# A Fourier mixer with a low-rank token mixer and an MLP: a new opening for batch 0, and a new plan for batches 1 and 2

## The chip, the cores and the metric

The kernel runs on one core of a Trainium2 chip. The core has a matrix engine (TensorE, PE), a vector engine (VectorE, DVE), an engine for activations and copies (ScalarE, ACT), a general one (GpSimd, POOL), and a queue engine (SyncE, SP) that only issues DMAs. Each runs its own instructions in order and waits on semaphores. The time is the device time of one execution in microseconds; the number given is the median of the runs.

## The reference, cut to what matters

```python
X = np.fft.rfft(x, axis=1)                  # x: 8 x 3136 x 256, along the 3136 tokens
Y = X * (filt_r + 1j * filt_i)[None]        # filters: 1569 x 256
y = np.fft.irfft(Y, n=3136, axis=1)
h = y.transpose(0, 2, 1) @ U @ V            # rank 32, U: 3136 x 32, V: 32 x 3136
u = y + h.transpose(0, 2, 1)
out = u + np.maximum(u @ w_ch1, 0) @ w_ch2  # 256 -> 1024 -> 256
```

Inputs and output are float32; the kernel computes in float16 with float32 accumulation.

## The kernel before, in words

The 3136 tokens are 64 q by 49 r, and both transforms are done as matmuls in two factors, so that each batch goes through four stages. **Step 1** (`st1`, lines 262 to 290) multiplies x by a 64-point transform, 13 pieces for each batch, and stores the result in the DRAM tensor `ct1`. The **middle stage** loads tiles `a2` (98 rows, eight tiles k of four frequencies each) from `ct1`, applies the 49-point transform (`stage2`, two matmuls with `w2t`), multiplies by the filter, applies the inverse 49-point transform (`stage3`), casts to `esb` and stores to `ct2`. The filter product has two forms. In the first, `fa` and `fc` hold rearranged copies of the filters; three products and a sum give `y`, and stage 3 needs one matmul for each half tile. In the second, stage 2 is done with two weight sets, one product with `fb` as loaded gives `uv`, and stage 3 adds two matmuls for each half tile. **Low rank** (`low_rank`, `low_rank_end`) multiplies `esb` by the transformed U (`uh`, from `u_hat`) to a 32-row `h1`. **Stage 4** (`stage4`) takes `e2`, 64 rows of the middle result read back from `ct2` with `h1` beneath them as rows 64 to 95 (`put_h`), and multiplies by `sv`, which holds the inverse 64-point transform and V, to the transposed tokens `ut` of one group. Then the MLP: `mm1`, a ReLU on ScalarE into a ring `hring`, `mm2_part`, the residual, `och` and the output.

There are six groups of 512 tokens for each batch and one of 128 for each pair of batches. The last loop runs over groups and eight steps t in each: `mm1` of group n, at two of the steps `stage4` of group n+1, and a quarter or half of `mm2` of group n-1. Into these steps a table written by hand (`plan`, `early`) puts everything that the next batches need: `plan_mid` the middle stage, `plan_st1` step 1, `plan_rest` the loads of `e2`, low rank and `put_h`. A step number counts over all groups; batch 1's groups start at step 48. The tables set the order within each engine, and nothing reorders it at run time.

Before the loop, batch 0 takes a path of its own. Step 1 stays on the chip: `turned` writes it transposed into `cm`, `turn_a2` transposes it back into the tiles that stage 2 wants, and `mid_first` runs 16 half tiles j in the second form of the product, four of them on GpSimd. After it come low rank, all of step 1 of batch 1, and stage 4 of group 0. In this version `cm` is the memory of `fc`, so that the rearranged filters (`make_fa`) are made after batch 0.

Loads that convert float32 to float16 are issued by GpSimd (x, filters, U, V, `w1sb`, `w2sb`). In the order of the built program each of them waits until the one eight places ahead of it has landed. SyncE issues the others, in order; a load from `ct1` or `ct2` waits there for the stores that it reads, and everything behind it waits as well. [...]

Of the kernel before, what the change touches and what calls it, by code (L numbers as in the profile page):

```python
# [24 lines left out]
def _consts():  # L25
# [10 lines left out]
    wf = np.zeros((128, 25, 128))  # L36
    for h in range(2):
        wf[h::2, 0:24, 64 * h:64 * h + 64] = t1[:, 24 * h:24 * h + 24]
    wf[0:64, 24, 0:64] = t1[:, 48]
# [59 lines left out]
    return (wf.reshape(128, 25 * 128).astype(f16), w2.astype(f16), g3.astype(f16),  # L99
# [4 lines left out]
def kernel(  # L104
# [13 lines left out]
    names = ("wf", "w2", "g3", "s4", "su", "tw", "kr")  # L118
    wf_d, w2_d, g3_d, s4_d, su_d, tw_d, kr_d = (
# [22 lines left out]
    def bank(tag):  # L142
        of = {"m": (0, 1), "o": (2, 3), "w": (4,), "e": (7,), "f": (0, 1, 2, 3, 4, 7), "e0": (7, 4), "f0": (0, 1), "w1": (7, 5, 6)}[tag]
        turn[tag] = turn.get(tag, -1) + 1
        return psum[:, of[turn[tag] % len(of)], :]


    NH = 17
    hring = cst.tile([128, NH, 512], F16, name="hring")
# [3 lines left out]
    wf = cst.tile([128, 25, 128], F16, name="wf")  # L153
    for c in range(4):
        i = slice(8 * c, min(8 * c + 8, 25))
        nc.sync.dma_start(wf[:, i], wf_d.rearrange("p (i m) -> p i m", m=128)[:, i])
# [3 lines left out]
    def load_x(b, c, after=None):  # L160
# [3 lines left out]
        else:  # L164

            t = sb.tile([128, 4, XW], F16, tag="x", bufs=4, name="x")
            if after is not None:
                nc.gpsimd.tensor_copy(t[0:1, 0, 0:1], after[0:1, 0:1])
# [10 lines left out]
    def load_filters(a, z):  # L179
# [8 lines left out]
        if z == NK:  # L188
            for p0, src in ((0, filt_r), (64, filt_i)):
                nc.gpsimd.dma_start(fb[p0 + 25:p0 + NR, 31, :],  # L190
                                    dram(src.tensor, 32 * DM, [[64 * DM, 24], [1, DM]]))
            nc.gpsimd.dma_start(fb[0:25, 31, :], dram(filt_r.tensor, 0, [[64 * DM, 25], [1, DM]]))
            nc.gpsimd.dma_start(fb[65:89, 31, :],
                                dram(filt_i.tensor, 64 * DM, [[64 * DM, 24], [1, DM]]))
            nc.gpsimd.dma_start(fb[64:65, 31, :],
                                dram(filt_r.tensor, 1568 * DM, [[DM, 1], [1, DM]]))

    zero = cst.tile([128, 64], F16, name="zero")
    nc.vector.memset(zero, 0.0)
    nc.vector.memset(fb[96:128], 0.0)  # L200
    nc.scalar.copy(fb[32:64].rearrange("p s (k f) -> p (s k) f", f=64),
                   free(zero, 32, 64, 0, [[0, NK * DM // 64], [1, 64]]))
    nc.vector.memset(fc[:, 24:29, :], 0.0)
    usb = hflat[0:64, 0:NR * RANK]
    nc.gpsimd.dma_start(usb, moe_U.rearrange("(q r) p -> q (r p)", q=NQ))
# [4 lines left out]

# [7 lines left out]
    nc.scalar.dma_start(g3, g3_d.rearrange("p (f m) -> p f m", f=6))  # L218

# [3 lines left out]
    w2sb = cst.tile([128, 8, DM], F16, name="w2sb")  # L223
    vnat = hflat[64:96, 4704:4704 + SEQ]
    nc.gpsimd.dma_start(vnat, moe_V)
    nc.gpsimd.dma_start(w1sb, moe_w_ch1.rearrange("(h dd) c -> dd h c", h=2))

    sv = cst.tile([96, SEQ], F16, name="sv")
    kr = cst.tile([128, 96], F16, name="kr")

    def keep_warm(n):
        z = bank("f")
        for _ in range(n):
            nc.tensor.matmul(z, wf[:, 0, :], wf[:, 0:4, :].rearrange("p i m -> p (i m)"),
                             start=True, stop=True)
# [4 lines left out]
    def u_hat():  # L240
        ud = hflat[0:64, 1568:4704].rearrange("q (p c r) -> q p c r", c=2, r=NR)
        for p, eng in ((0, nc.vector.tensor_copy), (16, nc.scalar.copy)):
            eng(ud[:, p:p + 16], bass.AP(tensor=usb.tensor, offset=usb.offset + p,
                                         ap=[list(usb.ap[0]), [1, 16], [0, 2], [RANK, NR]]))
        for p in range(0, RANK, 8):
            z = bank("f")
# [4 lines left out]
            t = [sb.tile([98, NK, 8], F32, tag=tag, bufs=3, name="ut") for tag in ("ta", "tb")]  # L251
# [8 lines left out]
    def st1(b):  # L260
        for c in range(3):
            asb = sb.tile([128, 8, DM], F16, tag="asb", bufs=3, name="asb")
            for j in range(4):
                pf = bank("w" if b > 1 else "w1")
# [5 lines left out]
                if b == 1 and j % 2:  # L270
                    nc.vector.tensor_copy(dst, pf)
                else:
                    nc.scalar.copy(dst, pf)  # L273
                if j < 3:
                    yield
            for h in range(2):
                nc.sync.dma_start(dram(ct1[b], (16 * c + h) * 64 * DM,
                                       [[DM, 64], [128 * DM, 8], [1, DM]]), asb[64 * h:64 * h + 64])
            if 1 < b < NB - 1 and c:
                load_x(b + 1, c - 1)  # L280
            yield
        pf = bank("w" if b > 1 else "w1")
        nc.tensor.matmul(pf[0:64, 0:DM], wf[0:64, 24, 0:64], xt[b, 3], start=True, stop=True)
        al = sb.tile([64, DM], F16, tag="al", bufs=2, name="al")
        nc.scalar.copy(al, pf[0:64, 0:DM])
        nc.sync.dma_start(dram(ct1[b], 48 * 64 * DM, [[DM, 64], [1, DM]]), al)
        if 1 < b < NB - 1:
            load_x(b + 1, 2)
            load_x(b + 1, 3)
        yield  # L290


    cm = fc.rearrange("p s d -> p (s d)")

    def turned(c):
        for g in range(0, 8 if c < 3 else 1, 4):
# [268 lines left out]
    for n, _ in enumerate(st1(1)):  # L565
        if n == 3:
            low_rank_end(0)
# [200 lines left out]
```

## Time and profile before

| | us |
|---|---|
| median of 10 runs | 557.36 (552.26 to 560.26) |
| profiled execution | 557.31, span 555.5 |
| TensorE busy | 517.3 (93%) |
| ScalarE, VectorE, GpSimd busy | 391.0, 352.8, 282.3 |
| first stage 3 cast (`esb`) of batch 0 | 29.89 |
| last stage 3 cast of batch 0 ends | 50.47 |
| first `mm1` of group 0 | 61.36 |
| first `mm1` of step 8 (group 1) | 72.20 |
| `e2` of batch 1 there, first `stage4` on it | 130.34 |

Times within the execution count from the start of the span. The chain is followed back from the last instruction to what released each one. A wait of an engine that is not on that chain costs nothing by itself. [...]

### The profile page before, as it was taken

The page shows a single profiled execution, that of the slowest core. Times are in us where ns is not written, and L with a number is a line of the kernel's source. Part 1 is how long each engine was busy: PE and PEld are TensorE (multiplying, and loading weights), DVE is VectorE, ACT ScalarE, POOL GpSimd, SP SyncE. Part 2 cuts the span into 40 slices and gives each one's busy share as a digit, 9 for nine tenths or more (in the row PEclk, how much of TensorE's full clock was granted, in tenths as well). Part 3 has the DMA queues.
Part 4 walks back from the last instruction along what each step waited for, and adds up shares of the span by engine and source line. Part 5 has one row for each costly group of instructions (what it writes and reads, how often), then busy time and mean ns, then how long its engine had stood idle before and what let it go on. Part 6 is the DMA issues. An engine that isn't in the chain of part 4 may idle for free.

```text
span 555.5 us, 11638 instructions
## 1 busy us (share of the span) xinstructions
PE 517.3 (93%) x4491; PEld 375.5 (68%) x4491; DVE 352.8 (64%) x409; ACT 391.0 (70%) x684; POOL 282.3 (51%) x194
## 2 busy tenths in 40 slices
PE   4967689996999999999999999999999999999996
PEld 2634356664767777677776777677786777777775
DVE  6654775755756686758746785858746887643332
ACT  8566868774787687767876788667777577765663
POOL 5678179951884065915683175806563297300000
PEclk8798899997999999999999999999999999999999
DMA  9998986894679467774879468765653554343212
GB/s 188 162 163 174 241 151 185 209 229 131 169 186 246 129 174 198 172 200 141 200 220 221 123 173 225 165 197 155 188 170 120 141 167 121 106 113 114 96 77 87
DMA packets 85433, 92.06 MB, mean 166 GB/s; under 512 B 6742, under 2 KB 69417, under 8 KB 85377
## 3 DMA queue, kind: packets, MB, share of 16 engines
q1 hardware_dynamic: 67968, 75.12, 45.8%
q0 software_dynamic: 16960, 15.91, 19.1%
q8 instruction: 35, 0.57, 0.4%
q10 hardware_dynamic: 448, 0.28, 0.3%
q14 instruction: 22, 0.17, 0.1%
HBM read 57.42 MB, written 49.77 MB: 193 GB/s over the span
## 4 chain that ended last, share of the span: by engine, by line
PE 70%; POOL 10%; DMA 7%; DVE 7%; ACT 3%; issue 2%; DVEq 0%; ACTq 0%; POOLq 0%; SPq 0%
PE psum L521 25%; PE psum L488 24%; PE psum L352 4%; PE psum L344 4%; PE psum L477 4%; PE psum L497 3%; PE psum L266 3%; POOL y L634 3%; DMA x<-in_x_dram 3%; POOL x L170 2%; DVE ut L482 1%; DMA w1sb<-in_moe_w_ch_dram 1%; DVE tb L632 1%; PE psum L416 1%; DMA ct<-esb 1%
## 5 line engine op out<-in xcount | busy, mean ns | idle before, releaser
L492 ACT ACTIVATE hring<-psum 128x512 f16<-128x512 f32 (+1 forms) x416 | 237.7, 576 | 103.1 <-PE psum L488 101.9
L488 PE MATMUL psum<-ut,w1sb 128*128 128x512 f16 (+1 forms) x832 | 240.9, 371 | 4.5 <-DVE ut L482 2.1
L521 PE MATMUL psum<-w2sb,hring 128*128 128x256 f16 x1536 | 231.0, 273 | 0.0
L634 POOL TENSOR_TENSOR y<-ta,tb 128x1024 f16<-128x1024 f16 x56 | 120.6, 2160 | 159.5 <-DVE tb L632 113.5
L521 PEld LDWEIGHTS <-hring 128*128 128x128 f16 x1536 | 143.4, 98 | 62.9 <-issue 3.0
L482 DVE CAST ut<-psum 128x512 f16<-128x512 f32 x96 | 71.0, 740 | 107.1 <-PE psum L477 86.8
L488 PEld LDWEIGHTS <-w1sb 128*128 128x128 f16 x832 | 104.7, 145 | 26.9 <-issue 10.2
L529 DVE COPY och<-psum 128x512 f32<-128x512 f32 x96 | 66.2, 689 | 47.3 <-PE psum L497 46.7
L326 ACT CAST esb<-psum 98x512 f16<-98x512 f32 x128 | 74.8, 587 | 22.6 <-PE psum L344 17.0
L628 DVE TENSOR_TENSOR ta<-psum,fb 128x1024 f16<-128x1024 f32 x41 | 50.0, 1219 | 7.9 <-PE psum L352 6.9
L273 ACT CAST asb<-psum 128x512 f16<-128x512 f32 x78 | 45.9, 589 | 12.4 <-PE psum L266 11.3
L497 PE MATMUL psum<-idn,ut 128*128 128x128 f16 x392 | 54.0, 219 | 0.0
L477 PEld LDWEIGHTS <-e 96*128 96x128 f16 x768 | 35.9, 98 | 25.6 <-issue 10.3
L630 DVE TENSOR_TENSOR tb<-psum,fc 64x1024 f16<-64x1024 f32 x41 | 50.3, 1226 | 0.9
L632 DVE TENSOR_TENSOR tb<-psum,fc 64x1024 f16<-64x1024 f32 x41 | 49.9, 1218 | 0.8
L477 PE MATMUL psum<-sv,e 96*128 96x64 f16 x768 | 38.8, 194 | 6.6 <-DMA e<-ct 3.8
L344 PE MATMUL psum<-y,g 128*98 128x512 f16 x105 | 39.9, 380 | 3.0 <-POOL y L634 1.6
L497 PEld LDWEIGHTS <-ut 128*128 128x128 f16 x392 | 38.5, 98 | 4.9
L628 POOL TENSOR_TENSOR ta<-pc,fb 128x1024 f16<-128x1024 f16 x15 | 32.4, 2157 | 10.8 <-ACT pc L638 10.8
L352 PE MATMUL psum<-a,w2t 98*128 98x512 f16 x113 | 34.7, 383 | 2.1 <-DVE tb L632 1.6
L266 PE MATMUL psum<-x,wf 128*128 128x256 f16 x168 | 32.4, 284 | 2.0 <-ACT asb L273 0.6
L630 POOL TENSOR_TENSOR tb<-pc,fc 64x1024 f16<-64x1024 f16 x15 | 31.8, 2122 | 1.2
(93 smaller groups left out, 371.0 us busy)
## 6 DMA issues: line engine op xcount, KB each, us to landing
out_dram<-och SPq DMA_DIRECT2D x47, 512.0 KB
ct<-esb SPq DMA_DIRECT2D x64, 196.0 KB
x<-in_x_dram POOLq DMA_DIRECT2D x48, 256.0 KB, 8.4
e<-ct SPq DMA_DIRECT2D x48, 256.0 KB
a<-ct SPq DMA_DIRECT2D x56, 196.0 KB
ct<-asb SPq DMA_DIRECT2D x42, 256.0 KB
wf<-wf SPq DMA_DIRECT2D x3, 256.0 KB
w1sb<-in_moe_w_ch_dram POOLq DMA_DIRECT2D x1, 512.0 KB, 7.7
```

The costliest lines, as they stand in the source:

```text
L326: nc.scalar.copy(esb[b, k][:, 2 * half:2 * half + 2, :].rearrange("p s d -> p (s d)"), pe[0:98])
L344: nc.tensor.matmul(pe[0:98], g3[:, m, :], v, start=(n == 0), stop=(n == len(parts) - 1))
L477: nc.tensor.matmul(pu[:, 64 * i:64 * i + 64], e2[b, c][:, i, 128 * dh:128 * dh + 128], sv[:, 64 * r:64 * r + 64], start=(i == 0), stop=Tru ...
L482: nc.vector.tensor_copy(o, v)
L488: nc.tensor.matmul(ph[:, 0:n], w1sb[:, dh, :, t], gr.ut[:, dh, 0:n], start=(dh == 0), stop=(dh == 1))
L492: nc.scalar.activation(h[:, 0:n], ph[:, 0:n], RELU)
L497: nc.tensor.matmul(o[:, dh * 128:dh * 128 + 128], gr.ut[:, dh, t0:t0 + n], idn, start=False, stop=(dh == 1), skip_group_check=True)
L521: nc.tensor.matmul(o, gr.h[tt][:, i * 128:(i + 1) * 128], w2sb[:, tt, :], start=(tt == 0), stop=False, skip_group_check=True)
L529: nc.vector.tensor_copy(gr.och[:, 2 * y:2 * y + 2, :].rearrange("p j d -> p (j d)"), gr.pc)
L628: eng.tensor_mul(ta, p, va)
L630: eng.tensor_mul(tb[0:64], p[64:128], vb[64:128])
L634: nc.gpsimd.tensor_add(ys[k], ta, tb)
```

## The change

It has these parts.

- **Constants.** U is loaded by SyncE as float32, and so is `wfc`, a compact form of the step 1 weights from which VectorE builds `wf` with two multiplications. `sv` and `kr` are loaded later. Two constants are new: `sel` and `s4x`.
- **Rows.** Filter products, `y`, `uv` and stage 3 work on 113 rows (NZ) instead of 128. `tb` becomes three fixed tiles whose rows 32 to 63 are zeroed once.
- **cm** is memory of its own, so `fc` can be filled during batch 0: `make_fc` on GpSimd, `make_neg` on VectorE, `make_fa` once batch 1 no longer needs `fb` as loaded.
- **Opening.** `turned` and `u_hat` alternate, and the warm-up matmuls read a zeroed part of `cm`.
- **mid_first.** Only half tile 12 goes to GpSimd; low rank is added up tile by tile; the last filter row is loaded behind `w1sb`; V is reordered by GpSimd between the loads of the first and second third of x of batch 1.
- **Group 0.** Rows 0 to 47 of `e2` come from `ct2`. The other 16 rows are picked from `esb` by 32 selection matmuls (`pick`), into rows that are then multiplied by `s4x`; V times `h1` is a third matmul into the same PSUM tile.
- **Step 1 of batch 1.** Three of its pieces stand in `mid_first`, ten in steps 0 to 7 of the loop. Its odd row (`xl`) is loaded ahead of the last third of x, and `w2sb` behind both. Its last stores are issued by GpSimd.
- **Plan.** Batch 1's middle stage takes tiles in the order 0, 3, 1, 5, 2, 4, 6, 7, four of them in the second form. x of batch 2 is loaded when `a2` of tile 0 has landed, x of batch 3 at steps 40 to 45. Batch 2's middle stage starts at step 44 instead of 39, with its first loads at step 41 instead of 31.

```diff
-    wf = cst.tile([128, 25, 128], F16, name="wf")
-    for c in range(4):
-        i = slice(8 * c, min(8 * c + 8, 25))
-        nc.sync.dma_start(wf[:, i], wf_d.rearrange("p (i m) -> p i m", m=128)[:, i])
+    usb = hflat[0:64, 0:2 * NR * RANK].bitcast(F32)
+    nc.sync.dma_start(usb, moe_U.rearrange("(q r) p -> q (r p)", q=NQ))
+    wfc = hflat[:, 6272:6272 + 1604]
+    nc.sync.dma_start(wfc, wf_d)
...
+    cm = cst.tile([128, 7232], F16, name="cm")
+    nc.vector.memset(cm[:, 2 * SEQ:], 0.0)
...
+    for h in range(2):
+        nc.vector.tensor_scalar_mul(wf[:, :, 64 * h:64 * h + 64],
+                                    wfc[:, 0:1536].rearrange("p (i m) -> p i m", m=64),
+                                    wfc[:, 1600 + 2 * h:1602 + 2 * h].bitcast(F32))
...
+    def make_fc(k, copy):
+        copy(fc[0:NR, 4 * k:4 * k + 4], fb[64:NZ, 4 * k:4 * k + 4])
+
+    def make_neg(k):
+        nc.vector.tensor_scalar_mul(fc[64:NZ, 4 * k:4 * k + 4], fb[64:NZ, 4 * k:4 * k + 4], -1.0)
+
+    def make_fa(k, copy):
+        copy(fa[64:NZ, 4 * k:4 * k + 4], fb[0:NR, 4 * k:4 * k + 4])
...
+        def low_rank_part(k):
+            for i in range(4):
+                a = 4 * k + i
+                nc.tensor.matmul(ph[32 * i:32 * i + 32], uh[:, a, :], esb[0, k][:, i, :],
+                                 start=(k == 0), stop=(k == 7), skip_group_check=True)
...
+        def pick(j):
+
+            for i in range(2):
+                sl = 2 * (j - 12) + i
+                for g in range(4):
+                    nc.tensor.matmul(zp[32 * g:32 * g + 32], sel[:, g, 28 - 4 * sl:60 - 4 * sl],
+                                     esb[0, j // 2][:, 2 * (j % 2) + i, :], start=(sl == 0),
+                                     stop=(sl == 7), skip_group_check=True)
...
+                if k == 5:
+                    load_e2(0, 0, 48)
+                if k == 6:
+                    load_e2(0, 1, 48)
+                if k == 7:
+                    load_e2(0, 1, 64, 48)
+                    nc.sync.dma_start(sv[0:64, 512:], s4_d[:, 512:])
+                    load_e2(0, 2)
+                    load_e2(0, 6)
...
-        for c in range(4):
-            load_x(1, c)
-        nc.gpsimd.dma_start(w2sb, moe_w_ch2.rearrange("(cc t) e -> cc (t e)", t=8))
+        load_x(1, 0)
+        nc.gpsimd.tensor_copy(sv[64:96, :].rearrange("p (r q) -> p r q", q=NQ),
+                              vnat.rearrange("p (q r) -> p r q", q=64))
+        load_x(1, 1)
...
-            if j in (7, 9, 12, 14):
...
+            if j == 12:
+                pc = sb.tile([NZ, 2, 2 * DM], F16, tag="pc", bufs=2, name="pc")
+                nc.scalar.copy(pc, pz[0:NZ])
                 nc.gpsimd.tensor_mul(uv, pc, fin)
+                for k in (3, 2, 5):
+                    make_fc(k, nc.gpsimd.tensor_copy)
             else:
...
+                nc.vector.tensor_mul(uv, pz[0:NZ], fin)
+            if j < 6:
+                turn_a2(j + 2)
             todo.append((j, uv))
-            if len(todo) > 3:
+            while len(todo) > (3 if 11 < j < 15 else 2) or todo and j == 15:
                 do3(*todo.pop(0))
...
+        step1(1)
+        step1(1)
+        pick(14)
+        low_rank_part(7)
+        pick(15)
+        h1[0] = hp = sb.tile([128, DM], F16, tag="hp", bufs=1, name="hp")
+        nc.vector.tensor_copy(hp, ph)
+        zs = sb.tile([128, DM], F16, tag="zs", bufs=1, name="zs")
+        nc.scalar.copy(zs, zp)
+        keep_warm(2, psum[:, 7, :])
+        low_rank_end(0)
...
+                nc.tensor.matmul(pu[dh][:, 64 * i:64 * i + 64],
+                                 e2[0, 0][0:48, i, 128 * dh:128 * dh + 128],
+                                 sv[0:48, 64 * i:64 * i + 64], start=(i == 0), stop=False,
+                                 skip_group_check=True)
+        for dh in range(2):
+            nc.tensor.matmul(pu[dh], zs[:, 128 * dh:128 * dh + 128], s4x, start=False, stop=False,
+                             skip_group_check=True)
+        step1(1)
+        for dh in range(2):
+            nc.tensor.matmul(pu[dh], h1[0][64:96, 128 * dh:128 * dh + 128], sv[64:96, 0:512],
+                             start=False, stop=True, skip_group_check=True)
...
     mid_first()
+    keep_warm(3, psum[:, 7, :])
+    load_x(1, 3)
+    load_x(1, 2)
+    nc.gpsimd.dma_start(w2sb[:, :, 0:DM], moe_w_ch2.rearrange("(cc t) e -> cc t e", t=8))
+    for k in (4, 0, 1, 6, 7):
+        make_fc(k, nc.gpsimd.tensor_copy)
+    put_h(0, 1)
...
+            for k, q in ((0, 11), (3, 11), (1, 11), (5, 11), (2, 17), (4, 20), (6, 22), (7, 25)):
+                at(q, fetch, k)
+            for k, q, d in ((3, 17, 26), (5, 21, 31), (2, 23, 33), (4, 28, 37)):
+                at(q, two, k)
...
+            for k, qs in ((0, (15, 16)), (1, (19, 20)), (6, (33, 34)), (7, (36, 37))):
+                for half, q in enumerate(qs):
+                    at(q, two_q, k, half)
+                    early[q + 1].append((mul_q, (k, half)))
+                    at(q + (3 if k == 7 else 2), three_q, k, half)
+            return 40
...
+    for n in (0, 0, 1, 1, 2, 3, 4, 5, 6, 7):
+        at(n, step1, 1)
+    at(13, lambda: load_x(2, 0, a2q[0][0:1, 0:1]))
+    for c in range(4):
+        if c:
+            at(13 + c, load_x, 2, c)
+        at((40, 42, 44, 45)[c], load_x, 3, c)
...
-            plan_st1(b, 12, (0, 1, 3, 4, 5, 7))
+            plan_st1(b, 18, (0, 3, 4, 5, 7))
...
-        m = later(start[b - 1], (5, -9, -12)[min(b, 3) - 1])
-        z = plan_mid(b, m, (2, 5) if b > 1 else (1, 3, 5))
+        m = later(start[b - 1], (16, -4, -12)[min(b, 3) - 1])
+        z = plan_mid(b, m, (2, 5) if b > 2 else (1, 3, 5))
```

## The prediction

> **What bounds the kernel now.** I read the slices of the page first, then busy time by stretch, then the chain that ended last, then the waits of TensorE, then the instructions in order of time. Two rows of the page (40 slices of 13.9 us; busy share and granted clock of TensorE, in tenths):
>
> ```profile
> PE   4967689996999999999999999999999999999996
> PEclk8798899997999999999999999999999999999999
> ```
>
> From the eleventh slice on TensorE is full at full clock; losses sit in the first six slices and in the tenth. By stretch (us; busy us and count on PE, PEld, DVE, ACT, POOL; clock; DMA share; GB/s):
>
> ```profile
> 0.00:14.00 14.00, 6.44 (x42) 3.73 (x42) 9.62 (x12) 11.16 (x3) 7.74 (x16) 0.84 0.97 188
> 28.00:42.00 14.00, 9.76 (x44) 4.63 (x43) 8.35 (x8) 8.18 (x13) 10.99 (x14) 0.94 1.00 165
> 56.00:70.00 14.00, 9.30 (x60) 4.81 (x59) 10.96 (x18) 11.76 (x14) 3.02 (x6) 0.87 0.92 236
> 126.00:140.00 14.00, 9.76 (x71) 6.34 (x70) 6.84 (x9) 5.89 (x11) 2.30 (x2) 0.76 0.53 145
> 140.00:200.00 60.00, 58.51 (x526) 43.26 (x525) 40.56 (x47) 44.15 (x85) 33.35 (x21) 1.00 0.70 176
> ```
>
> After 140 us TensorE is the bound, and the change hardly touches that work. So the time is: when the group pipeline starts, plus the TensorE work from there, plus stalls before 140 us. The chain (start, length, what) names them:
>
> ```profile
> 5.06 14.35 DMA x<-in_x_dram
> 37.29 0.57 POOL w2sb L384
> 37.87 2.14 POOL uv L397
> 40.05 0.73 PE psum L344 x2
> 48.77 0.61 PE psum L344 x2
> 49.40 0.59 ACT esb L326
> 58.62 1.46 PE psum L234 x6
> 60.35 0.74 DVE ut L482
> 119.92 6.46 DMA ct<-esb
> 126.52 3.68 DMA e<-ct
> ```
>
> x of batch 0 is not in until 19.7. At 37 GpSimd stands at its load of w2sb (3.00 us, until w1sb has landed), so product 7 is late and TensorE idles 3.39 us. The last esb ends at 50.47. Step 1 of batch 1 then runs before group 0, whose first mm1 stands at 61.36, its second half at 62.34. In the loop one wait of TensorE is long, at the turn to batch 1, and matmuls are slow afterwards:
>
> ```profile
> PE psum L477 <- DMA e<-ct: 3.8, 1, 3.8
> ```
> ```profile
> 50.50 0.31 SPq L329 DMA_DIRECT2D ct<-esb  x1
> 53.83 1.11 SPq L438 DMA_DIRECT2D e<-ct  x2
> ```
> ```profile
> 125.37 0.60 PE L521 MATMUL psum<-w2sb,hring 128*128 128x256 f16 x4
> 130.73 1.04 PE L521 MATMUL psum<-w2sb,hring 128*128 128x256 f16 x4
> ```
>
> The SyncE pair shows the price of the round trip through DRAM: 3.33 us from a store to the load that waits for it, 3.7 us more for the load (126.52 to 130.34).
>
> [...] 1.04 for 0.60 us after the wait at 130, until 135.9. [...] The products here take 2.12 us for 1024[...].
>
> **Part by part**, all against this execution (557.31 us, span 555.5; the 1.8 us around it stay; the median of the runs is 557.36).
>
> *Until the first product.* U goes to SyncE (0.74 us less ahead of x on GpSimd), wf is half as large and sv and kr come later: by tile sizes 1.27 MB of constants instead of 1.9 with U. x was 3.2 MB, so 5.1 MB (f32) came in 18.2 us; 0.63 MB less is 2.2 us at that rate, 3 with the earlier issue: x complete near 16.7. But turned and u_hat now alternate on TensorE: 16 turned matmuls 1.9 us (twice) and 1.2, u_hat 1.5+0.75+0.65, warm-up 1.6, from x's first third at 11.5 to 20.5. u_hat's last products and sum on VectorE (1.5), the a2 copy (0.69) and two matmuls (0.43) follow: product 0 at 23.2 instead of 25.45. **-2.2.** The two multiplications that build wf (a 64x2048 scaling takes 0.68) and three memsets (0.5 each) end by 10.5, hidden by x.
>
> *Middle stage of batch 0.* Now 15 products go to VectorE at 1.2, one a2 copy at 0.69, and only product 12 to GpSimd. 113 rows for 128 cost the same[...]. Six rounds also turn a tile: 1.01+0.59 us on ScalarE, so about 1.45 us a round; then 1.2: 23.2+8.7+7.2 is 39.1 after product 11; 13, 14, 15 end at 43.2. Stage 3, two casts and the bank wait put the last esb at 44.5. Before 50.47: **-3.8 more**, the 3.4 us stall at 37 and half a microsecond. GpSimd must be free for product 12 at 39.5: last filters near 26, V reordered 27.5 to 34.5 (6.93), the load of x's second third behind it issued by 35.8. Hidden by 4 us.
>
> *Closing group 0.* Rows 0 to 47 of e2 come from DRAM, 48 to 63 from selection matmuls on esb. These are 32 of the kind of low_rank (32 in 1.06 us), most while TensorE waits. esb of product 11 ends at 41.8; store 3.3 and load 3.7 put e2 at 48.8. [...] I take 47.7. After it 16 matmuls of 64, four of 512, one step 1, three warm-ups and a cast 0.74: 2.4 us at full clock (0.5, 0.86, 0.22, 0.74), 4.4 at half; I take 4.3, since TensorE has stood still before. Full mm1 at 52.0 instead of 62.34. Sum so far **-10.3**, with ends -15 and -8.
>
> *Group 0.* Before, 9.9 us to step 8, with make_fa on ScalarE (3.7) and VectorE in it. Now 10 of 13 pieces of step 1: eight evictions on VectorE 0.69 each, two ut 0.74, put_h, and make_neg, of which three come before step 8 at about 0.35: 9.0 us. **-0.9.** Queued on GpSimd behind product 12: fc copies 3, 2, 5, then x's odd row, the last third, w2sb, five more fc copies, then ct1's last stores. A copy: [...] 2.26 by sv's reorder (6.93 for 3136). [...]
>
> *Steps 8 to 46 of batch 0.* Four of eight k use the two-product form: 16 more matmuls of 512, 3.45 us at 0.216 (pairs of mm1 follow each other in 0.43). VectorE gives up 1.2 us for each and GpSimd two pooled products. a2 of batch 1 waits for ct1's stores on GpSimd: eviction near 60.5, issue and receipt 4.5, load 3.5: 69 against step 15 near 68.5. x of batch 2 is issued only when a2 has landed: 69.5 plus 6 to 8.4, against step 19 near 75.5: 1.5 us late. Against this, half of the four or so microseconds of small waits between 72 and 126 may go: **+3.0** (1.5 to 6).
>
> *Turn to batch 1.* The last stage 3 stays at step 40. a2 of batch 2 is now fetched at step 41 and used at 44, queued on SyncE behind the e2 load that waits for the last ct2 store. The wait moves from e2 at step 46 to a2 at step 44: store 3.3 to 6.5, issue 1, load 3.5, less 5.5 us of steps. That is 2.3 to 5.5 where 3.8 stood: **0** (-2 to +2). Out of cover, each late microsecond counts in full. Batch 2's middle stage has 0.9 us of stage 2 less behind it: **+0.9.** It ends 11 units (512 tokens by one of eight steps) before batch 2's groups, where before it was 14; later batches have 12 and show no such wait: 0.
>
> Sum: -10.3-0.9+3.0+0+0.9 = -7.3; span 548.2, time **550**.
>
> **Rivals.** *A: the start gained is kept and the turn is cheap* (e2 not late, clock full[...]): start 47.5, no late x, turn 3 less: -17, 541. For it: DMA is lighter around 42; against: every round trip measured so far took 7 us. *B: waits in the loop take back the head*: x of batch 2 and a2 each 2 to 3 us late and half clock after each: 556, within half a per cent. For it: both are chained behind GpSimd stores with no slack. *C, slower: GpSimd's queue.* Three fc copies stand ahead of the last third and all eight ahead of ct1's stores, so step 15 moves by eight times a copy's excess over about 1.7 us, and step 4 by three. At 2.26 that is 4.5 us; the gain is gone at 2.6, half a per cent is lost at 3.0: 562. For it: shifting 64 rows down is a form that the trace doesn't show on GpSimd; against: the two-input product takes only 2.12. *D: nothing moves, as the pipeline's start is hidden*: excluded, since after 140 TensorE has no idle time in which a late start could be made up.
>
> **The numbers.** Forecast 0.5 (546 to 555), A 0.22, B 0.16, C 0.12. The range reaches into A and to the end of B: 539 to 560. Faster by over 0.5% (below 554.6; about what a measurement can tell from no change) 0.74, within 0.5% 0.14, slower 0.12.
>
> **What would show it.** Right: first ut cast near 51, no idle time near 37, mm1 of step 8 near 61, four matmuls per k more at the new stage 2 and 3, a TensorE wait for a2 at step 44 and none for e2 at 46. Wrong: first mm1 before 49 (e2's round trip cheaper than 7 us) or after 55; fc copies above 2.3; a wait for x at step 4 or step 19 above 3 us; a new wait at the start of batch 2's groups.

## The result: 1.2% slower, at the turn to batch 1

The changed kernel takes 562.86 us (median of 14 runs, 560.86 to 567.06) against 556.99 us for the kernel before (median of 51, 552.26 to 561.26). The ratio is 1.0116, with a 95% interval of 1.0093 to 1.0140. A ratio here is taken between fast runs alone and so need not be the quotient of the two medians. The forecast was 550.0, so the sign is wrong. The profiled execution of the changed kernel took 561.2 us, its span 559.3 us.

The slices of the changed kernel (40 of 14.0 us; busy share and granted clock of TensorE, in tenths):

```profile
PE   5896889938998999999999999999999999999996
PEclk9899899988999999999999999999999999999999
```

Slices three and five, both 6 before, are 9 and 8 now. But the ninth slice, 112 to 126 us, holds a 3; the worst that the kernel before had at its turn to batch 1 was a 6, one slice later.

By stretch, for the changed kernel (us; busy us and count on PE, PEld, DVE, ACT, POOL; clock; DMA share; GB/s):

```profile
0.00:14.00 14.00, 8.19 (x60) 4.96 (x60) 9.64 (x13) 6.67 (x7) 9.37 (x18) 1.00 0.96 194
28.00:42.00 14.00, 13.20 (x87) 5.69 (x86) 11.59 (x10) 9.11 (x15) 12.67 (x7) 1.00 0.93 177
42.00:56.00 14.00, 9.64 (x94) 5.21 (x94) 6.37 (x9) 6.51 (x12) 9.07 (x11) 1.00 1.05 188
56.00:70.00 14.00, 12.08 (x98) 8.45 (x95) 12.06 (x24) 7.10 (x12) 1.91 (x2) 0.88 0.57 153
112.00:124.00 12.00, 4.88 (x61) 3.54 (x60) 2.11 (x4) 3.57 (x7) 1.94 (x4) 0.87 0.89 173
124.00:136.00 12.00, 7.37 (x49) 4.56 (x49) 5.58 (x7) 2.93 (x6) 0.00 (x0) 0.70 0.54 115
```

The part that the change was about went better than forecast: from 28 to 42 TensorE works 13.20 of 14 us, where it worked 9.76. The loss is in the last two rows, 12.25 us of work in 24 us, the second half of it at a mean clock of 0.70. The kernel before did 18.95 us of work between the same times.

TensorE's longest waits in the changed kernel (what stood, releaser: total, times, longest), and then SyncE's and GpSimd's issues around the worst of them:

```profile
PE psum L399 <- DMA a<-ct: 12.3, 2, 10.0
PE psum L265 <- DVE cm L220: 5.8, 1, 5.8
PE psum L599 <- DMA sv<-s: 2.5, 1, 2.5
```
```profile
110.93 0.56 SPq L658 DMA_DIRECT2D out_dram<-och  x1
112.56 0.32 SPq L376 DMA_DIRECT2D ct<-esb  x1
121.70 0.48 SPq L559 DMA_DIRECT2D e<-ct  x1
122.23 0.59 SPq L559 DMA_DIRECT2D e2l<-ct  x1
122.99 1.31 SPq L362 DMA_DIRECT2D a<-ct  x3
```
```profile
110.94 2.46 POOL L187 DMA_DIRECT2D x<-in_x_dram  x4
113.36 0.58 POOL L180 DMA_DIRECT2D xl<-in_x_dram  x1
```

The last ct2 store of batch 1 leaves at 112.56, and the e2 load that waits for it is issued at 121.70. The time between these two issues is called the receipt of the store from here on. It is 9.1 us, where the kernel before needed 6.6 (119.92 to 126.52). The three a2 loads of batch 2 stand behind that load on the same queue. In the 1.6 us ahead of the store and the 1.4 us after it, GpSimd sends the loads of x(3,1), x(3,2) and xl of batch 3, four times 256 KB and 32 KB. SyncE has just sent 512 KB of output. In the kernel before those loads of x left at 109.4 to 112.4, 7.5 us ahead of the store.

What TensorE saw of it, in order of time (start, length, instruction, idle time before it and its releaser):

```profile
45.56 0.64 PE L517 MATMUL psum<-sv,e 48*128 48x64 f16 x16 [0.85 <-DMA e<-ct]
...
55.72 0.39 PE L599 MATMUL psum<-sv,e 96*128 96x64 f16 x8 [2.47 <-DMA sv<-s]
70.44 0.59 PE L399 MATMUL psum<-a,w2t 98*128 98x512 f16 x2 [2.36 <-DMA a<-ct]
...
126.84 1.01 PE L399 MATMUL psum<-a,w2t 98*128 98x512 f16 x2 [9.96 <-DMA a<-ct]
...
128.93 1.06 PE L643 MATMUL psum<-w2sb,hring 128*128 128x256 f16 x4
...
135.68 0.60 PE L643 MATMUL psum<-w2sb,hring 128*128 128x256 f16 x4
```

The wait of 0.85 us at 45.56 is all that TensorE sees of group 0's round trip through DRAM. The wait of 9.96 us ends at 126.84. After it the same four matmuls take 1.06 us and not 0.60, until about 131. The granted clock is 1.00 at the start of the wait, 0.50 from 121 to 131.2, and 1.00 again from 131.3.

The lead of the changed kernel over the kernel before, read at the same step of the loop in both traces, tells where the time went (us; negative is ahead; for group 0 of the kernel before, the second half of its first mm1 is taken):

```
first full mm1 of group 0     48.10 against  62.34   -14.2
mm1 of step 8                 60.02 against  72.20   -12.2
mm1 of step 44               115.83 against 123.42    -7.6
first stage 4 of batch 1     130.85 against 130.34    +0.5
its fourth full group        168.15 against 168.15     0.0
batch 2's second group       205.93 against 202.55    +3.4
last stage 4                 539.73 against 535.97    +3.8
```

14.2 us are won at the opening. Then 6.6 are lost between group 0 and step 44, 8.1 at the turn, and 3.4 in the half batch before batch 2's groups.

This is one execution of each kernel, and their starts differ from one execution to the next. In the traces of five kernels with the new opening (the changed one and the first four of the experiments below) the first full mm1 of group 0 stands at 46.92 to 49.14 and the mm1 of step 44 at 115.83 to 117.70. In three with the old opening these stand at 59.74 to 62.34 and at 119.83 to 123.42. The pair in the table has the earliest step 44 of the five against the latest of the three. Taken between the means, the lead is 12.6 us at group 0 and 4.6 at step 44. With the 8.1 us of the turn and 2.9 from there to batch 2's second group that makes a kernel 6.4 us slower, which is what the ratio says (6.5 us); the pair of traces alone gives 3.8.

### The profile page after: what moved, and what is told of

It reads as the page before. It is cut to its first block, busy times and chain, and to the rows that moved or that the text cites. A ratio compares the mean times of both kernels' runs of the same rounds, so it can differ in the third digit from the quotient of the medians.

```text
span 559.3 us, 11736 instructions
## 1 busy us (share of the span) xinstructions
PE 519.4 (93%) x4540; PEld 375.2 (67%) x4540; DVE 353.0 (63%) x413; ACT 375.6 (67%) x678; POOL 283.7 (51%) x204
## 4 chain that ended last, share of the span: by engine, by line
PE 55%; POOL 5%; ACT 1%; DVE 1%; issue 1%; ACTq 0%; POOLq 0%
PE psum L643 21%; PE psum L610 21%; PE psum L619 3%; PE psum L599 3%; PE psum L391 3%; PE psum L399 3%; PE psum L304 2%; POOL y L743 2%; POOL x L187 1%; PE psum L537 1%; POOL tb L741 1%; POOL ta L737 1%; POOL tb L739 1%; ACT esb L369 0%; DVE ut L604 0%
## 5 line engine op out<-in xcount | busy, mean ns | idle before, releaser
L743 POOL TENSOR_TENSOR y<-ta,tb 113x1024 f16<-113x1024 f16 x52 | 112.4, 2168 | 160.3 <-DVE tb L741 103.7
L604 DVE CAST ut<-psum 128x512 f16<-128x512 f32 x94 | 69.7, 742 | 98.8 <-PE psum L599 85.6
L737 DVE TENSOR_TENSOR ta<-psum,fb 113x1024 f16<-113x1024 f32 x37 | 45.1, 1218 | 17.8 <-issue 9.8
L399 PE MATMUL psum<-a,w2t 98*128 98x512 f16 x120 | 37.1, 386 | 16.1 <-DMA a<-ct 12.3
L739 DVE TENSOR_TENSOR tb<-psum,fc 49x1024 f16<-49x1024 f32 x37 | 45.4, 1226 | 1.0
L741 DVE TENSOR_TENSOR tb<-psum,fc 49x1024 f16<-49x1024 f32 x37 | 45.1, 1218 | 1.0
L599 PE MATMUL psum<-sv,e 96*128 96x64 f16 x752 | 37.8, 193 | 3.2 <-DMA sv<-s 2.5
L391 PE MATMUL psum<-y,g 113*98 113x512 f16 x98 | 37.4, 381 | 2.9 <-POOL y L743 1.6
L737 POOL TENSOR_TENSOR ta<-pc,fb 113x1024 f16<-113x1024 f16 x15 | 32.3, 2156 | 10.5 <-ACT pc L747 10.4
L739 POOL TENSOR_TENSOR tb<-pc,fc 49x1024 f16<-49x1024 f16 x15 | 31.8, 2119 | 1.2
```

The source lines that it names most:

```text
L391: nc.tensor.matmul(pe[0:98], g3[0:NZ, m, :], v, start=(n == 0), stop=(n == len(parts) - 1))
L599: nc.tensor.matmul(pu[:, 64 * i:64 * i + 64], e2[b, c][:, i, 128 * dh:128 * dh + 128], sv[:, 64 * r:64 * r + 64], start=(i == 0), stop=Tru ...
L604: (nc.scalar.copy if gr is groups[0] and dh else nc.vector.tensor_copy)(o, v)
L737: eng.tensor_mul(ta, p[0:NZ], va)
L739: eng.tensor_mul(tb[0:NR], p[64:NZ], vb[64:NZ])
L743: nc.gpsimd.tensor_add(ys[k], ta, tb)
```

## The experiments

The theory, called T in the expectations: at the turn the loads of x collide with the last ct2 store and stretch its receipt, and all that SyncE holds behind the waiting e2 load is late. Its rivals: the order on SyncE, or the output store ahead, is the cause by itself (O); or the loss is the added work of the loop and the stall only shows where it ends (W). Gains below that are worked out from two ratios are the difference of the ratios to the kernel before, times 557 us; every group of runs had its own runs of the kernel before beside it.

**x of batch 3 held back.**

```
-        at((40, 42, 44, 45)[c], load_x, 3, c)
+        if c == 1:
+            at(42, lambda: load_x(3, 1, e2[1, 0][0:1, 0, 0:1]))   # GpSimd waits for e2(1,0)
+        else:
+            at((40, 42, 44, 45)[c], load_x, 3, c)
```

> Only the loads of x(3,1), x(3,2) and xl of batch 3 change: they are held on GpSimd until e2(1,0) has landed. Theory T (these five loads, 0.8 MB issued at 110.9 to 113.4, stretch the receipt of the last ct2 store of batch 1, issued at 112.6, from some 3.5 to 9.1 us, and everything queued on SyncE behind it is late): the receipt falls to 3.5 to 5 us, TensorE's wait for a2 at step 44 from 10.0 to 4 or 5 us, time 5 to 6 us below the changed kernel. Rival O (the order on SyncE and the 512 KB store of the output ahead make the receipt long anyway): receipt above 7.5 us, wait above 8 us, time within 1.5 us of the changed kernel.

Measured: 554.73 us, ratio 0.9964 (0.9936 to 0.9993), 8.5 us below the changed kernel by the two ratios. SyncE's two issues, and TensorE's wait:

```profile
113.80 0.32 SPq L376 DMA_DIRECT2D ct<-esb  x1
116.49 0.48 SPq L559 DMA_DIRECT2D e<-ct  x1
```
```profile
121.31 1.01 PE L399 MATMUL psum<-a,w2t 98*128 98x512 f16 x2 [3.20 <-DMA a<-ct]
```

The store comes back in 2.7 us with the output store and the order on SyncE as they were, and the wait falls from 10.0 to 3.2 us. Rival O falls. The gain is larger than T said, and the receipt fell below the 3.5 us that T gave it. (The five loads are 1.1 MB as written, not the 0.8 of the expectation.) The profiled span is 5.5 us shorter than the changed kernel's (553.8 against 559.3), with 2.3 us more of the wait for sv in it (4.8 against 2.5).

**a2 of batch 2 fetched ahead of the waiting e2 load.**

```
-            at(later(s, -3 if b == 2 else -9), fetch, k)
+            at(later(s, -5 if b == 2 else -9), fetch, k)
```

> Only the fetch of the first three a2 tiles of batch 2 moves, from step 41 to step 39, so that on SyncE it stands ahead of the e2 load that waits for the last ct2 store. Theory T: a2 is there at step 44, the wait moves to e2 at step 46, about 3 us of work later, with the receipt still 8 to 9 us: 6.5 to 7.5 us instead of 10.0; time 2 to 3.5 us below the changed kernel. Rival O (the order on SyncE is the whole of the loss at the turn): the wait falls below 4 us and the time by 6 us or more. Rival W (the loss is the extra work of TensorE and the later middle stage of batch 2, the stall only takes the place of others): within 1.5 us of the changed kernel.

Measured: 559.55 us, ratio 1.0056 (1.0034 to 1.0078), 3.3 us below the changed kernel. TensorE at the turn:

```profile
120.71 1.01 PE L399 MATMUL psum<-a,w2t 98*128 98x512 f16 x2 [2.80 <-DMA a<-ct]
...
129.35 0.59 PE L599 MATMUL psum<-sv,e 96*128 96x64 f16 x8 [5.03 <-DMA e<-ct]
```

The order costs what T said and no more. The store, now sent at 115.06, took 10.8 us to come back (e2 issued at 125.84). The 10.0 us became 2.8 for a2, which waits for the last ct1 store of batch 2, and 5.0 for e2.

**Both edits together.**

> Both edits: x(3,1), x(3,2), xl held until e2(1,0) has landed, and the a2 fetch at step 39. Theory T: store receipt 3.5 to 5 us, e2 lands about 119.5 against a need at about 118.5: a wait of 0 to 2 us in all, no half clock around 121 to 131, time 9 to 11 us below the changed kernel, so 552 to 554 and below the kernel before. Rival W: the gain is given back in steps 46 to 104 as other waits, time at most 4 us below the changed kernel.

Measured: 553.40 us, ratio 0.9940 (0.9913 to 0.9967), 9.8 us below the changed kernel and below the kernel before. Its issues on SyncE and its longest waits other than the first warm-up's:

```profile
113.58 1.22 SPq L362 DMA_DIRECT2D a<-ct  x3
114.84 0.39 SPq L376 DMA_DIRECT2D ct<-esb  x1
118.70 0.49 SPq L559 DMA_DIRECT2D e<-ct  x1
```
```profile
PE psum L599 <- DMA sv<-s: 3.5, 1, 3.5
PE psum L599 <- DMA e<-ct: 2.7, 1, 2.7
PE psum L399 <- DMA a<-ct: 2.1, 1, 2.1
```

The gain is of the size that T gave. W, which gave at most 4 us, falls: nothing of the gain is taken back later, the trace is 8.5 us ahead of the changed kernel at the first stage 4 of batch 1 (122.36 against 130.85) and 8.4 at the last (531.33 against 539.73). What W named is there beside it: from that first stage 4 to batch 2's second group e3 takes 75.19 us, the changed kernel 75.08 and the kernel before 72.21. One detail of the expectation was wrong. The waits did not fall to 2 us or less but to 4.8, because SyncE stood at the a2 fetch until ct1's receipt at 113.58 and let the ct2 store go only at 114.84.

**The output store moved behind the turn.** The 512 KB that SyncE sent at 110.9 are kept in a list and sent at step 42, behind the a2 fetch.

```
+                def store(och=gr.och):
+                    nc.sync.dma_start(dram(out.tensor, o, ...), och)
+                (held.append if gr is groups[3] else lambda f: f())(store)
...
+    at(42, lambda: held.pop()())
```

> Only the 512 KB store of the output of batch 0's group 3, issued at 110.9 on SyncE just ahead of the last ct2 store of batch 1, moves behind the a2 fetch (step 42). Theory T: it is one of two loads on the DMA engines at that moment and the smaller one; the receipt falls by 1 to 3 us, time 1 to 3 us below the changed kernel. Rival O: this store is what the ct2 store queues behind; the receipt falls below 5 us and the time by 5 us or more. Lower bound: no change, if the loads of x alone fill the engines.

Measured: 559.78 us, ratio 1.0074 (1.0039 to 1.0109), 2.3 us below the changed kernel. The last ct2 store and the e2 load behind it:

```profile
114.43 0.32 SPq L376 DMA_DIRECT2D ct<-esb  x1
122.72 0.49 SPq L559 DMA_DIRECT2D e<-ct  x1
```

The receipt is 8.3 us where 9.1 stood, and the wait for a2 8.8 where 10.0 stood. O's 5 us are not there. The output store has at most a small share: its 0.8 us of receipt is less than the 1 to 3 that T gave it, and the 2.3 us of time are hardly clear of noise, as the two intervals overlap (1.0039 to 1.0109 and 1.0093 to 1.0140).

**The same collision put into the kernel before, and taken out of it.** First, its loads of x(3,1), x(3,2) and xl moved to just ahead of the last ct2 store, and nothing else.

```
-            if 1 < b < NB - 1 and c:            (and the second such line; b > 2 in both)
+    for c in range(4):
+        at((20, 40, 41, 42)[c], load_x, 3, c)
```

> The kernel before with one part of the change alone: its loads of x(3,1), x(3,2) and xl of batch 3 leave GpSimd behind two more sums, at about 116.7 to 119.7 instead of 109.4 to 112.4, just ahead of its last ct2 store at 119.9. Theory T: the receipt of this store grows from 6.5 to 8.5 to 10 us, TensorE's wait for e2 from 3.8 to 6 to 8 us, and the time by 2 to 5 us. Rival (the order on SyncE is what made the receipt long): receipt and time stay, within 1 us.

Measured: 556.80 us, ratio 1.0032 (1.0010 to 1.0055), 1.8 us more than the kernel before beside it. Its last ct2 store and the e2 load behind it, and the wait:

```profile
116.33 0.32 SPq L329 DMA_DIRECT2D ct<-esb  x1
124.99 0.51 SPq L438 DMA_DIRECT2D e<-ct  x1
```
```profile
PE psum L477 <- DMA e<-ct: 5.8, 1, 5.8
```

The loads left at 110.9 to 114.0, 2.3 us or more ahead of the store, so the collision is milder than meant: 8.7 us of receipt where 6.6 stood, 5.8 us of wait where 3.8 stood. The time went up by just less than T's 2 us. Then the other way, the same loads held until e2(1,0) has landed:

```
+    at(27, load_x, 3, 0)
+    at(43, lambda: load_x(3, 1, e2[1, 0][:, 0, :]))
+    for c in (2, 3):
+        at(43, load_x, 3, c)
```

> The kernel before, with x(3,1), x(3,2) and xl of batch 3, issued at 109.4 to 112.4 there and landing after some 10 us, held until e2(1,0) has landed. Theory T says that the same collision, in a weaker form, is in the kernel before: the receipt of its last ct2 store falls from 6.5 to 4 or 5 us, the wait of 3.8 us for e2 to 1 to 2 us, and 2 to 4 us are gained against the kernel before. Rival O (the 512 KB output store ahead of it is what counts there): receipt above 6 us and no gain (within 1 us).

Measured: 554.91 us, ratio 0.9962 (0.9939 to 0.9985), 2.1 us less than the kernel before.

```profile
117.60 0.31 SPq L329 DMA_DIRECT2D ct<-esb  x1
122.02 0.51 SPq L438 DMA_DIRECT2D e<-ct  x1
```

Receipt 4.4 us, wait 1.5. In this kernel x(3,0) left at 106.3 instead of 97.3 too, and TensorE later waited 1.5 us for x. So the cause does not belong to the change alone: it was in the kernel before with about 2 us, and the change made it large.

**sv loaded earlier.** This tests the wait of 2.5 us at step 4.

```
-                    nc.sync.dma_start(sv[0:64, 512:], s4_d[:, 512:])      (at k == 7)
+                if k == 4:
+                    nc.sync.dma_start(sv[0:64, 512:], s4_d[:, 512:])
```

> On the changed kernel, only the load of sv[0:64, 512:] moves on SyncE from behind the second load of e2(0,1) to the end of product k = 4, ahead of the first e2 load. Theory S (in group 0 stage 4 of step 4 waits for this load alone, because it stands behind a load that waits for the receipt of the last ct2 store of batch 0): the 2.5 us wait for sv goes, rows 48 to 63 of e2(0,1), issued at 50.9, are then 0.5 to 1.5 us late, and 1 to 2.5 us stay to the end. Rival: e2(0,1) is as late as sv, and nothing changes (within 0.7 us).

Measured: 563.39 us, ratio 1.0121 (1.0081 to 1.0160), no gain. The wait for sv is gone, but the wait for the first e2 grew from 0.85 to 2.2 us, and its load was issued at 43.56 and not 42.26. By the third group's first stage 4 the kernel was 0.7 us behind the changed one (62.99 against 62.31). So the gain is missing as the rival said, but by another way: e2(0,1) was not late, the first e2 was. The sizes vary between executions: in the eight traced kernels with sv late, the wait for sv is 1.6 to 4.8 us and that for the first e2 0.2 to 2.4, with its load issued at 41.0 to 43.0; in the three with sv early, the wait for the first e2 is 1.5 to 6.9 us, with its load at 43.4 to 44.5.

**Denser first stage of batch 2.** e3, with sv early, the first stage of batch 2 in six of eight steps and the a2 fetch at step 37.

```
-            plan_st1(b, 18, (0, 3, 4, 5, 7))
+            plan_st1(b, 18, (0, 1, 3, 4, 5, 7))
```

> The two edits of e3 and the early sv load, and first-stage pieces of batch 2 in six of eight steps instead of five, so that they end at step 35, not 37, with the a2 fetch of batch 2 at step 37; batch 2's middle stage still begins at step 44. Theory T: in e3 SyncE stood at the a2 fetch until the receipt of ct1, so the last ct2 store left at 114.8 instead of 112.5 and TensorE still waited 2.1 us for a2 and 2.7 us for e2; both fall below 0.7 us each, and with sv the time is 4 to 6 us below e3, at 548 to 550. Rival: the denser first stage pushes other work of steps 19 to 36, and the gain is under 2 us.

Measured: 556.50 us, ratio 0.9994 (0.9967 to 1.0020), 3.0 us above e3 by the two ratios. The first stage caught up with its own x: a wait of 3.3 us for it, which e3 does not have. a2 was fetched at 113.59 all the same, 6.3 us after the last ct1 store was issued at 107.33; the last two ct2 stores left at 115.0 and 116.1. There is no gain, as the rival said; what it cost was mostly batch 2's first stage waiting for its own x, at 80.50.

**Batch 2's middle stage two units earlier.** First on top of the last kernel, then on e3 alone, with the a2 fetch at step 38.

```
-        m = later(start[b - 1], (16, -4, -12)[min(b, 3) - 1])
+        m = later(start[b - 1], (16, -6, -12)[min(b, 3) - 1])
```

> As e6, and batch 2's middle stage begins at step 42 instead of 44, so that it ends two units earlier before its groups. Theory L (the changed kernel loses 3.4 us between steps 80 and 104 because this stage runs late, and its last products and stage 2 are waited for): waits of TensorE in that stretch fall from about 3 us towards 1 us, and the time is 1 to 3 us below e6. Rival (the loss there is the work itself, or follows from where the stage stands to the groups at each step and not from its end): within 0.7 us of e6 or above it.

> e3 with batch 2's middle stage begun at step 42 instead of 44 and its a2 fetch at step 38. Theory L (3.4 us are lost from step 80 to 104 because this stage runs late): from the first stage 4 of batch 1 to that of batch 2 some 2 to 3 us less than in e3; but a2, which waits for ct1 until about 113.5, is now needed at step 42 (112.8), which costs 1 to 2.5 us; time 0 to 2 us below e3. Rival: that stretch takes as long as in e3, and the time is 1 to 2.5 us above e3.

Measured: 553.56 us, ratio 0.9916 (0.9881 to 0.9951), for the first, and 553.35 us, ratio 0.9963 (0.9938 to 0.9988), for the second. From the stage 4 of batch 1's fourth full group to that of batch 2's second, one row each of the changed kernel, the kernel before and the second of these (columns as above):

```profile
168.15:205.93 37.78, 34.58 (x324) 25.21 (x323) 30.20 (x31) 25.22 (x50) 16.12 (x12) 1.00 0.68 171
```
```profile
168.15:202.55 34.40, 33.57 (x322) 24.91 (x321) 24.84 (x28) 24.90 (x49) 9.27 (x8) 1.00 0.71 182
```
```profile
163.90:199.80 35.90, 33.75 (x322) 24.92 (x320) 24.84 (x28) 24.85 (x49) 11.87 (x10) 1.00 0.69 175
```

The 3.4 us that the changed kernel loses there are 1.0 us of matmuls and 2.4 us of idle time, with 5.4 us more on VectorE. Two units earlier, the stretch is 1.9 us shorter. From the first stage 4 of batch 1 to the same end it is 1.6 us shorter than in e3 (73.63 against 75.19), and 2.8 us shorter in the first pair of kernels (72.14 against 74.91). So theory L holds for the stretch, in both pairs, though 1.6 us is less than the 2 to 3 that it gave the second. In time it shows in the first pair only: e7 is below e6 by 0.8% in their ratios and by 2.9 us in their medians. The second kernel does not beat e3. a2 was fetched at 115.2, so the store left at 117.1, and e2 was waited for 4.1 us.

**x(3,0) held as well, and that with the two earlier edits of batch 2's stages (without the early sv).**

```
+        if c:
+            at(42, load_x, 3, c)
+        else:
+            at(42, lambda: load_x(3, 0, e2[1, 0][0:1, 0, 0:1]))
...
-            ... -54 if b == 3 else -60 ...
+            ... -50 if b == 3 else -60 ...
```

> e3 with x(3,0), 0.5 MB issued at 104.4, held behind e2(1,0) as well, and the first stage of batch 3 four units later to fit. Theory T goes on: x(3,0) stretches the receipt of the last ct1 store of batch 2 (issued 108.8, received 113.5), at which SyncE stands ahead of the last ct2 store; the receipt falls by 1 to 2 us, the waits for a2 (2.1) and e2 (2.7) by 2 to 3 us together, and the time by 1.5 to 3 us against e3. Rival: x(3,0) has landed by then, and nothing changes (within 0.7 us), or the later first stage of batch 3 costs 1 to 2 us.

> e11 with the first-stage pieces of batch 2 in six of eight steps from step 20, which end at step 36, its a2 fetch at step 38 and its middle stage from step 43. If T and L both hold: waits for a2 and e2 below 1 us each and 1 to 1.5 us won back before batch 2's groups: 3 to 5 us below e3, 549 to 551. Otherwise, as in e6, the denser first stage takes from one place what it gives at another: within 1 us of e3.

Measured: 555.69 us, ratio 0.9992 (0.9960 to 1.0023), and 555.97 us, ratio 0.9994 (0.9971 to 1.0016), so 2.9 and 3.0 us above e3 by the ratios. In the first the waits at the turn fell only from 4.8 to 3.6 us (a2 1.3, e2 2.3), and x came late at another place (2.1 us). In the second a2 and e2 took 1.6 and 4.2 us, x 2.3. Holding x(3,0) shortens the waits at the turn by 1.2 us, less than T said, and the receipt of ct1 that T had it stretch stayed at 4.5 us (108.35 to 112.87) where e3 has 4.8. So this part of T was wrong: x(3,0) is not what holds ct1. Batch 3's first stage then waits for x; both rivals come nearer than the theories, and both gave too little of the loss.

## Why the prediction was wrong

One table says it: the receipt of the last ct2 store of batch 1 (from its issue to that of the e2 load behind it) in nine kernels, and when the loads of x(3,1), x(3,2) and xl leave GpSimd, from the first's issue to the last's end, against that store's issue (us):

```
kernel                        x leaves                           receipt
changed                       1.6 ahead to 1.4 after              9.1
changed, output later         1.6 ahead to 1.4 after              8.3
changed, a2 first             3.1 to 0.1 ahead                   10.8
changed, sv early             1.6 ahead to 1.4 after              9.5
before, x later               5.4 to 2.3 ahead                    8.7
before                        10.5 to 7.5 ahead                   6.6
before, x held                after e2 has landed                 4.4
changed, both edits           after e2 has landed                 3.9
changed, x held               after e2 has landed                 2.7
```

In the five later kernels that hold these loads it is 3.6 to 5.0 us. What the DMA engines moved just after the store does not tell the two ends of the table apart. The first 2.7 us, in the changed kernel and with x held (columns as above):

```profile
112.56:115.26 2.70, 2.70 (x46) 1.98 (x44) 0.00 (x0) 1.52 (x4) 1.38 (x3) 1.00 1.01 257
113.80:116.50 2.70, 2.70 (x46) 1.96 (x44) 0.00 (x0) 1.52 (x4) 0.00 (x0) 1.00 0.70 238
```

They moved 257 and 238 GB/s. But their busy share was 1.01 and 0.70, and GpSimd was sending loads in the first stretch only. How the engines divide their time among the queues no run shows, so by what way these loads hold up the store stays open.

Point by point, by the steps of the prediction:

- *Until the first product, -2.2.* Right, and more: -3.9, as the first product began at 21.53 and not 23.2.
- *Middle stage of batch 0, -3.8 more.* Right: -3.4. The stall at 37 is gone and the last esb ends at 43.15 (forecast 44.5). That 113 rows cost the same as 128 holds for this product on VectorE: `uv` over 1024 elements a row takes 1.218 us at 113 rows and 1.221 at 128 in the kernel before.
- *Closing group 0, full mm1 at 52.0, sum -10.3.* Mechanism right, size too small: -14.2 in this pair of traces, -12.6 between the means. e2 landed at 45.56 instead of 47.7, which was the author's estimate, 1.1 us below the 48.8 of the prediction's own sum. From there to mm1 it took 2.5 us and not 4.3, because the granted clock was 1.00 (from 42 to 56); the prediction had taken it as nearly half. (Its own terms at half clock, with the cast unchanged, add up to 3.9 and not to its 4.4.)
- *Group 0, -0.9.* Wrong by 2.9 us: 11.9 us to step 8 (48.10 to 60.02), not 9.0. 2.5 us of it is the wait for sv, with a granted clock of 0.50 behind it from 56.2 to 59.4 (0.88 from 56 to 70). The load of sv stands on SyncE behind a load that waits for a ct2 receipt of 7.3 us (43.56 to 50.88). The prediction listed GpSimd's queue for this stretch and left SyncE's out. The experiment shows that moving this load alone wins nothing. This receipt looks like the one at the turn: GpSimd sends xl, the last third of x and w2sb from 42.36 to 45.09, around the store at 43.56. No run moved these loads, so the likeness is not shown to be the cause.
- *The copies on GpSimd, rival C.* Three took 2.99 us and five 5.43, so 1.0 to 1.1 us each. That is less than half of the 2.26 that the prediction scaled from sv's reorder, and far below the 2.6 to 3.0 at which C decided. C's direction and its 562 came out, but by another way, so this is luck (at 3.0 us a copy C's own working gives 560).
- *Steps 8 to 46, +3.0.* 4.6 us to step 44 in this pair of traces, inside its range of 1.5 to 6. a2 was late by 2.4 us at 70.44; x of batch 2 was not.
- *Turn to batch 1, 0 (-2 to +2).* **This is the step that failed.** It named the right wait: a2 at step 44, queued behind the e2 load. Its sum was store 3.3 to 6.5, issue 1, load 3.5, less 5.5 us of steps: 2.3 to 5.5. Measured: 9.1 + 1.3 + 3.85, less 4.3 of steps (112.56 to 116.88), which is 10.0. Of the 6.1 us above the middle of that sum the receipt is 4.2 and the shorter cover 1.2. The receipt was taken from two receipts of the kernel before, as if it belonged to the store. But the longer one, 6.6 by issues, was itself a receipt under load, as the experiment that holds x in the kernel before shows (4.4; with its load that round trip took 10.4 us, 119.92 to 130.34, and not the 7 that rival A gives for every one), and the change put the loads of x(3,1), x(3,2) and xl, at steps 42, 44 and 45, into the very window of the store. The prediction followed x of batch 2 through its chain, but never asked where these five loads of batch 3 would now stand against the store, and no rival did either. Against the kernel before, the wait is 6.2 us longer, and the granted clock of 0.50 behind it fell ahead of stage 4 of batch 1 (126.84 to 131.2, stage 4 at 130.85), where in the kernel before it came with stage 4 and after it (130.34 to 135.9), so that 8.1 us were lost there, half a microsecond of which came back by batch 1's fourth full group.
- *Batch 2's middle stage, +0.9 and later 0.* Wrong in size: 3.4 us. Its work was costed (1.0 us more matmul time in the stretch), but not that it now runs where VectorE has 30.2 of 37.8 us to do and TensorE waits for its products and sums (from 160 to 206 us 1.5 us for tb of VectorE and 0.9 for y of GpSimd). "11 units before its groups, where later batches have 12" was read as enough, and it was not.

With the turn mended, as in e3, the kernel is 0.6% or 3.3 us faster than the one before, on the side that was forecast, where 7.4 us were forecast. The forecast had 8.2 us of lead left at step 44, and between the means it was 4.6: the opening gave 2.3 us more than forecast, and group 0 and the steps up to 44 took 8.0 where 2.1 were forecast. So the turn is what failed by the most and what set the sign, but most of what e3 still lacks was lost ahead of it. The stage before batch 2's groups took 2 us more than its 0.9; the turn of e3 still held 4.8 us of waits, though from mm1 of step 44 to the first stage 4 it took 5.8 us, where the kernel before took 6.9. How much of the 2.4 us of idle time before batch 2 comes from VectorE's order and how much from the stage's end was not taken apart.

## What to carry to other kernels

A receipt read in a profile is the price of a store among the transfers of that moment, not of the store (2.7 to 10.8 us here for the same one). When a change moves a load that nothing gates, set its issue times beside the round trips that the critical path waits for, on all queues together, and if it falls into one, hold the load behind the arrival of what the path waits for; here that was worth 8.5 us in one kernel and 2 us in the other. On a queue that keeps order, whatever waits for a receipt should stand behind what does not: the a2 loads behind the waiting e2 load cost 3.3 us. And before a lead between two traces is read as a gain, look at other traces of the same opening; here they differ by 2 to 4 us at step 44.

## What the runs showed of the hardware

The same store of 196 KB in the same place came back after 2.7 to 10.8 us, depending on when GpSimd's loads left against it; with those held it was 2.7 to 5.0 us in all kernels that held them. Moving a single transfer or stage moved the wait and did not remove it three times: sv loaded earlier (2.5 us at step 4 became 1.4 more at the first e2), the denser first stage (3.3 us for x), and x(3,0) held (2.1 us for x). After the idle time of 10.0 us TensorE worked at a granted clock of 0.50 for 4.4 us (126.84 to 131.2; four matmuls in 1.06 us and not 0.60), and after the 3.8 us in the kernel before for about 5.5 (130.34 to 135.9; 1.04 and not 0.60). After the 2.5 us for sv it was 0.50 from 56.2 to 59.4. A copy of 49 rows by 1024 f16 elements that shifts 64 rows down took GpSimd 1.0 to 1.1 us, half of a two-input product of the same length (2.12).
